# GpSimd's short operations between the two parts of a step's scalings, and a free-axis sum in place of an addition

## The chip, the cores and the metric

The kernel runs on one core of a Trainium2 chip. The time is what the device needs for one execution, in microseconds (us). The kernel before was timed in three executions: 1083.58, 1084.55 and 1084.83 us, median 1084.55 us. One more execution was profiled; it took 1084.76 us, and the span of its own instructions is 1083.0 us. The granted TensorE clock was 0.999 in it.

## The reference

Eight batches of eight heads of causal attention with a decay, and then a feed-forward layer with a gate on the 4608 tokens that result:

```python
def _attn_ref(q, k, v, f):              # 8 x 8 x 576 x 64
    scores = scale * np.matmul(q, k.transpose(0, 1, 3, 2))
    cum = np.cumsum(np.log(np.clip(f, 0.0001, 1.0)), axis=-1)
    decay = cum[:, :, :, None] - cum[:, :, None, :]
    scores = np.where(causal, -1000000000.0, scores + decay)
    scores = scores - np.max(scores, axis=-1, keepdims=True)
    attn = np.exp(scores)
    attn = attn / (np.sum(attn, axis=-1, keepdims=True) + 1e-09)
    return np.matmul(attn, v)

def _moe_ref(x, w_in, w_out):           # 4608 x 512, 512 x 2048, 2048 x 512
    h = x @ w_in
    sp = np.maximum(h, 0.0) + np.log1p(np.exp(-np.abs(h)))
    return (h * erf(sp)) @ w_out
```

The attention's output, heads side by side, is the x of the layer.

## The kernel before

The first part of the program, about 340 us, is the attention; the rest is the layer, in 48 units that the change doesn't touch. The order of the instructions on every engine is the order in which the code names them.

**Steps.** The heads are taken in 32 pairs, each pair in two steps, so t runs from 0 to 63, with two more in which the pipeline empties. A head's 576 rows of scores are cut into five blocks of rows; an even step has blocks 4 and 1 (576 and 192 columns), an odd step blocks 3, 2 and 0 (448, 320 and 64 columns), each for both heads j of the pair. A tile of step t goes through five stages, one step apart:

- step t: `scores(t)` puts the products on TensorE (PE) into PSUM; a matrix on `upper` adds the causal mask to the rows' ends. `reduce(t, j)` (L559, VectorE, DVE) adds the decay `c`, writes `pr` and keeps each row's smallest value in `st[:, 0]`. The next step's `scores` needs the PSUM that `reduce` reads, of both heads.
- step t+1: `exps` (L571, ScalarE, ACT) writes the exponentials over `pr` and their sums into `st[:, 1]`.
- step t+2: `normalize` adds 1e-9 to the sums (L576, DVE), takes the reciprocal (L578, DVE), and GpSimd (POOL) scales each block by it (L582), large blocks first.
- step t+3: `transposes` (PE) turns `pr` in groups of up to four squares into one of three PSUM buffers `t`, and `evacuate` copies them to `pt` (ACT, and DVE for one group of an odd tile). For an odd tile the group with block 0 is turned first.
- step t+4: `values` (PE) multiplies with v into `o`, of which there is one buffer; one step later `store` (L630 and L633, DVE) copies it to `xo`, and a DMA writes it to `xt_d`. PE's `values` of a step waits for the `store` of the step's own round, which DVE does ahead of its `reduce`.

So PE's order in a step is s (scores of t), t (transposes of t-3), o (values of t-4), and DVE's is sums and reciprocal of t-2, store of t-5, reduce of t, and then the conversions.

**GpSimd's other work.** `mask(p, i)` (L546) writes a large negative value into a piece of the decay `c`. The one of block 4, for the next pair, stands in odd steps. The one of block 3, in even steps, overwrites columns that `reduce` of the same step has still to read, so it waits for DVE.

**Conversions.** Beside the attention the weights of the first units, and from step 23 on the first x, are cut into high and low parts. A list `work` with due times by step sets the pace, and `moe.later` that of x. Each entry, called by `convert` at the end of a step, has instructions on several engines: `words` and `joined` on DVE (L377 to L395, on 512 columns each), `out_high`, `in_high` and `high` on ACT (L401, L418, L138), and on GpSimd subtractions and additions of 256, 384 or 512 columns: `out_low` (L406), `combine` (L414), `in_low` (L424), `sub` (L132) and `low` (L143). These last are the short operations. `columns` counts GpSimd's columns of an entry. DMAs of the finished parts are issued on SyncE's queue (SP) ahead of the next entry.

Of the kernel before, what the change touches and what calls it, by code (L numbers as in the profile page):

```python
# [22 lines left out]
P = 128  # L23
# [38 lines left out]
X0 = 23  # L62
X1 = 60
BY_X0 = 17
NU1 = 4
# [5 lines left out]
EDGE = 24  # L71
# [243 lines left out]
def attention_moe(ctx, tc, q2, k2, vp, f, w_in, w_out, out):  # L315
# [19 lines left out]
    tiny = edge.tile([P, EDGE], F32, name="edge")  # L335
    nc.vector.memset(tiny, 1e-9)
# [124 lines left out]
    with ExitStack() as ph:  # L461
# [57 lines left out]
        def scores(t):  # L519
# [20 lines left out]
            line = wk.tile([P, 32], F32, name=f"st{t}", tag=f"st{half}")  # L540
            stats[t] = line[:, :6 * n].rearrange("p (a j m) -> p a j m", a=3, j=2)
# [32 lines left out]
        def normalize(t):  # L574
            st, n = stats.pop(t), len(BLOCKS[t % 2])
            nc.vector.tensor_tensor(out=st[:, 1], in0=st[:, 1], in1=tiny[:, :2 * n].rearrange("p (j m) -> p j m", j=2),  # L576
                                    op=ALU.add)
            nc.vector.reciprocal(out=st[:, 2], in_=st[:, 1])  # L578
            for m, i in enumerate(BLOCKS[t % 2]):
                for j in range(2):  # L580
                    seg = row(t, i, j)
                    nc.gpsimd.tensor_scalar(out=seg, in0=seg, scalar1=st[:, 2, j, m:m + 1], scalar2=1.0,  # L582
                                            op0=ALU.mult, op1=ALU.mult)

# [95 lines left out]
        for t in range(NH + 2):  # L680
# [13 lines left out]
            if there[2]:  # L694
                normalize(t - 2)
# [31 lines left out]
            if there[0] and not half:  # L727
                mask(p, 3)
            if t < 4:
                due = t + 1  # L730
            elif t <= X0:
                due = 4 + ((BY_X0 - 4) * (t - 3) + (X0 - 3) // 2) // (X0 - 3)
            else:
                due = BY_X0 + ((total - BY_X0) * (t - X0) + (X1 - X0) // 2) // (X1 - X0)
            while work and total - len(work) < due:
                done += columns(work[0])
                convert(work.pop(0))
            if t == X0:
                begun = done
            for _ in range(2 if t > X0 else 0):  # L740
                if moe.later and done < begun + (every - begun) * (t - X0) // (X1 - X0):
                    done += columns(moe.later[:1])
                    convert(moe.later[:1])
                    del moe.later[:1]
            if t > NH and there[4]:
                store(t - 4)
# [81 lines left out]
```

## Time and profile before

| | before |
|---|---|
| median of three executions | 1084.55 us |
| profiled execution, its own time | 1084.76 us |
| span of its instructions | 1083.0 us |
| PE busy in the span | 1071.5 us (99%) |
| DVE busy | 834.7 us (77%) |
| ACT busy | 745.7 us (69%) |
| GpSimd busy | 732.0 us (68%) |

Times in the rows are us from the start of the span, durations are us too, and nanoseconds where the view says so. A row of the timeline gives the start, the duration, the engine, the line, the operation, what it writes and reads, and how many instructions were merged into it; in square brackets stands how long the engine had been idle before it, and what ended that. PE's matmuls are pipelined and their ends are modelled, so PE's busy share hides its waits: an s row that waits in its midst is shown as a longer row.

### The profile page before, as it was taken

Reading aid. Unit: us, or ns where it says so; the run is one execution under the profiler, and the core shown is the slowest. Engines: PE = TensorE matmul, PEld = TensorE weight load, DVE = VectorE, ACT = ScalarE, POOL = GpSimd, SP = SyncE. Lnnn points to the kernel's source line nnn. Section 1 sums busy time; section 2 is a strip of 40 time slices with the busy share of each in tenths; the row PEclk is TensorE's granted clock in tenths of the full one; section 3 lists DMA queues with packets and bytes.
Section 4 is the critical chain, followed back from the end, with each engine's and each line's share of the span. In section 5 each row is a group of like instructions: output and inputs, shape, how many; then the busy total and the mean of one; then the engine's idle time right before and its main releaser. Section 6 shows DMA issues by size and latency. Waiting matters only on the chain.

```text
span 1083.0 us, 21938 instructions
## 1 busy us (share of the span) xinstructions
PE 1071.5 (99%) x7480; PEld 945.5 (87%) x7480; DVE 834.7 (77%) x1875; ACT 745.7 (69%) x1624; POOL 732.0 (68%) x887
## 2 busy tenths in 40 slices
PE   8999999999999999999999999999999999999998
PEld 6888887888889988998899888989998999899987
DVE  6898898888765997888887986685776768676665
ACT  5899888988987666657666666566476656656563
POOL 3777888988864969798787879636454555536322
PEclk9999999999999999999999999999999999999999
DMA  8799987899766597877969777785867768584742
GB/s 285 247 304 311 343 305 251 279 351 350 254 215 226 190 349 280 303 299 287 357 221 364 273 270 271 277 295 204 311 230 264 289 221 323 213 319 182 246 188 97
DMA packets 86191, 293.69 MB, mean 271 GB/s; under 512 B 8896, under 2 KB 25280, under 8 KB 73792
## 3 DMA queue, kind: packets, MB, share of 16 engines
q1 hardware_dynamic: 85936, 292.00, 75.9%
q8 instruction: 60, 0.98, 0.3%
q14 instruction: 51, 0.42, 0.1%
q10 hardware_dynamic: 144, 0.29, 0.1%
HBM read 240.73 MB, written 51.53 MB: 270 GB/s over the span
## 4 chain that ended last, share of the span: by engine, by line
PE 87%; DVE 4%; ACT 3%; DMA 3%; issue 1%; POOL 1%; SPq 0%; DVEq 0%; POOLq 0%; ACTq 0%
PE y L236 34%; PE pha L178 9%; PE phx L178 9%; PE phy L178 9%; PE s L528 7%; PE o L621 7%; PE t L594 5%; PE phb L178 4%; DMA xt_d<-xo 2%; ACT pr L571 1%; PE s L535 1%; POOL pr L582 1%; DVE pr L559 1%; DMA v<-in_vp_dram 1%; ACT pt L603 1%
## 5 line engine op out<-in xcount | busy, mean ns | idle before, releaser
L225 POOL TENSOR_TENSOR gl<-e,gh 128x384 fp32r<-128x384 f32 x192 | 218.2, 1168 | 262.7 <-PE y L236 162.4
L236 PE MATMUL y<-wo,gh 128*128 128x512 f32 x1152 | 356.5, 391 | 0.4 <-DVE ys L257 0.3
L236 PEld LDWEIGHTS y<-wo,gh 128*128 128x128 f32 x1152 | 215.0, 188 | 45.4 <-DVE ys L257 1.7
L236 PE MATMUL y<-wo,gl 128*128 128x512 f32 x576 | 225.1, 391 | 0.0
L257 DVE TENSOR_TENSOR ys<-y,ys 128x512 f32<-128x512 f32 x252 | 172.1, 687 | 55.2 <-PE y L236 53.6
L582 POOL TENSOR_SCALAR pr<-pr,st 128x576 f32<-128x576 f32 (+4 forms) x320 | 167.6, 544 | 49.2 <-ACT pt L603 11.9
L571 ACT ACTIVATE pr<-pr,st 128x576 f32<-128x576 f32 (+3 forms) x320 | 177.1, 560 | 2.2 <-DVE st L559 2.2
L559 DVE CUSTOM_DVE_ANT_0 pr<-s,c 128x576 f32<-128x576 f32 (+3 forms) x320 | 136.6, 487 | 40.9 <-PE s L535 18.4
L224 ACT CAST gh<-e 128x384 fp32r<-128x384 f32 x192 | 94.1, 513 | 67.3 <-DVE e L217 64.9
L207 ACT ACTIVATE e<-u 128x384 f32<-128x384 f32 x144 | 75.0, 523 | 78.2 <-DVE u L184 74.9
L236 PEld LDWEIGHTS y<-wo,gl 128*128 128x128 f32 x576 | 108.1, 188 | 22.8
L178 PE MATMUL pha<-xs,wi 128*128 128x384 f32 x576 | 117.0, 337 | 0.1
L178 PE MATMUL phx<-xs,wi 128*128 128x384 f32 x576 | 115.4, 334 | 0.0
L178 PE MATMUL phy<-xs,wi 128*128 128x384 f32 x576 | 115.3, 334 | 0.0
L528 PE MATMUL s<-k,q 64*128 64x320 f32 (+4 forms) x768 | 113.8, 407 | 1.5 <-DVE st L559 1.1
L603 ACT COPY pt<-t 128x512 f32<-128x512 f32 x158 | 88.6, 582 | 33.5 <-PE t L594 33.4
L207 ACT ACTIVATE e<-pha 128x384 f32<-128x384 f32 x48 | 23.6, 492 | 125.7 <-PE pha L178 125.7
L621 PEld LDWEIGHTS o<-pt,v 128*64 128x64 f32 x1920 | 93.7, 137 | 14.2 <-DVE st L559 6.9
L178 PEld LDWEIGHTS pha<-xs,wi 128*128 128x128 f32 x576 | 102.3, 188 | 4.2 <-DVE u L188 0.4
L621 PE MATMUL o<-pt,v 128*64 128x128 f32 (+1 forms) x1920 | 102.5, 259 | 3.1 <-DVE xo L630 2.9
L528 PEld LDWEIGHTS s<-k,q 64*128 64x128 f32 x768 | 75.0, 186 | 31.3 <-issue 16.0
L594 PE MATMUL t<-ident,pr 128*128 128x128 f32 x800 | 100.9, 275 | 1.3 <-ACT pt L599 0.9
(75 smaller groups left out, 1780.5 us busy)
## 6 DMA issues: line engine op xcount, KB each, us to landing
wi<-wi_d SPq DMA_DIRECT2D x48, 1792.0 KB, 7.5
wo<-wo_d SPq DMA_DIRECT2D x48, 1024.0 KB, 5.6
v<-in_vp_dram SPq DMA_DIRECT2D x32, 576.0 KB, 5.2
r<-xt_d SPq DMA_DIRECT2D x48, 384.0 KB, 8.9
c<-cum_d SPq DMA_DIRECT2D x62, 288.0 KB, 6.9
q<-in_q_dram SPq DMA_DIRECT2D x32, 320.0 KB, 5.7
k<-in_k_dram SPq DMA_DIRECT2D x32, 288.0 KB, 6.0
part_d<-ys SPq DMA_DIRECT2D x36, 256.0 KB, 6.0
```

Source lines behind the costliest of these rows:

```text
L178: nc.tensor.matmul(out=ps, lhsT=wi[:, w, n, kd], rhs=xs[:, x, kd], start=not part and kd == 0 and i == 0, stop=kd == 1 and i == 2, skip_gr ...
L207: nc.scalar.activation(out=e_, in_=h[c], func=AF.Softplus)
L225: nc.gpsimd.tensor_tensor(out=gl, in0=e_, in1=gh.bitcast(F32), op=ALU.subtract)
L236: nc.tensor.matmul(out=y, lhsT=x[:, cs], rhs=wo[:, i, w], start=i == 0 and n == 0, stop=i == 1 and n == 2)
L257: nc.vector.tensor_tensor(out=ys, in0=y, in1=ys, op=ALU.add)
L528: nc.tensor.matmul(out=s[j][:, at:at + k1 - k0], lhsT=q[h, PAD + START[i]:PAD + END[i]], rhs=k[h, k0:k1], start=i > 0, stop=k1 < END[i] or ...
L559: nc.vector.tensor_tensor_reduce(out=to[:, ::-1] if j else to, in0=score, in1=decay_, scale=-0.125, scalar=BIG, op0=ALU.add, op1=ALU.min, ...
L571: nc.scalar.activation(out=seg, in_=seg, func=AF.Exp, bias=st[:, 0, j, m:m + 1], scale=-1.0, accum_out=st[:, 1, j, m:m + 1])
L582: nc.gpsimd.tensor_scalar(out=seg, in0=seg, scalar1=st[:, 2, j, m:m + 1], scalar2=1.0, op0=ALU.mult, op1=ALU.mult)
L594: nc.tensor.transpose(out=b[:, n * P:(n + 1) * P], in_=probs[t][:, at:at + P], identity=ident)
L603: nc.scalar.copy(out=pt[:, 512 * a:512 * a + 512], in_=b)
L621: nc.tensor.matmul(out=o[h, to:to + width], lhsT=v[:, ch, h], rhs=pt[:, at[j]:at[j] + width], start=n == 0, stop=n == len(parts) - 1, skip ...
```

## The change

Two things are changed. The constant 1e-9 now stands beside the sums in the same tile `line`, and one instruction that sums over two neighbouring places (a tensor reduce along the free axis, on sums and constant) takes the place of the addition of two tiles. Four fixed tiles are used in turn, where a pool gave four before. And `normalize` is cut in two: the sums, the reciprocal and the large block (576 or 448 columns, both heads) stay at the start of a step; the smaller blocks come at its end. Where a step's entries have at most 640 columns (`SHORT`) for GpSimd, they are called ahead of block 3's mask and of the smaller blocks; otherwise behind them. Entries of x are no longer taken in the step in which their high part is made.

```diff
-    tiny = edge.tile([P, EDGE], F32, name="edge")
-    nc.vector.memset(tiny, 1e-9)
+    lines = [edge.tile([P, 2, 6 * len(BLOCKS[n % 2])], F32, name=f"line{n}") for n in range(4)]
+    for line in lines:
+        nc.vector.memset(line[:, 1], 1e-9)
...
-            line = wk.tile([P, 32], F32, name=f"st{t}", tag=f"st{half}")
-            stats[t] = line[:, :6 * n].rearrange("p (a j m) -> p a j m", a=3, j=2)
+            stats[t] = lines[t % 4][:, 0, :6 * n].rearrange("p (a j m) -> p a j m", a=3, j=2)
...
-        def normalize(t):
-            st, n = stats.pop(t), len(BLOCKS[t % 2])
-            nc.vector.tensor_tensor(out=st[:, 1], in0=st[:, 1], in1=tiny[:, :2 * n].rearrange("p (j m) -> p j m", j=2),
-                                    op=ALU.add)
-            nc.vector.reciprocal(out=st[:, 2], in_=st[:, 1])
-            for m, i in enumerate(BLOCKS[t % 2]):
+        def normalize(t, rest):
+            half = t % 2
+            st, n = stats[t], len(BLOCKS[half])
+            total = st[:, 2].rearrange("p j m -> p (j m)")
+            if not rest:
+                nc.vector.tensor_reduce(out=total, in_=lines[t % 4][:, :, 2 * n:4 * n].rearrange("p w c -> p c w"),
+                                        axis=mybir.AxisListType.X, op=ALU.add)
+                nc.vector.reciprocal(out=total, in_=total)
+            for m in range(n - 1, 0, -1) if rest else range(1):
                 for j in range(2):
-                    seg = row(t, i, j)
+                    seg = row(t, BLOCKS[half][m], j)
                     nc.gpsimd.tensor_scalar(out=seg, in0=seg, scalar1=st[:, 2, j, m:m + 1], scalar2=1.0,
                                             op0=ALU.mult, op1=ALU.mult)
+            if rest:
+                del stats[t]
...
-                normalize(t - 2)
+                normalize(t - 2, False)
...
-            if there[0] and not half:
-                mask(p, 3)
...
+            todo = []
             while work and total - len(work) < due:
-                done += columns(work[0])
-                convert(work.pop(0))
+                todo.append(work.pop(0))
...
             for _ in range(2 if t > X0 else 0):
-                if moe.later and done < begun + (every - begun) * (t - X0) // (X1 - X0):
-                    done += columns(moe.later[:1])
-                    convert(moe.later[:1])
+                last = todo[-1][0][0] if todo and todo[-1] else None
+                if last != moe.high and moe.later and (
+                        done + sum(map(columns, todo)) < begun + (every - begun) * (t - X0) // (X1 - X0)):
+                    todo.append(moe.later[:1])
                     del moe.later[:1]
+            now = sum(map(columns, todo))
+            done += now
+            for late in (False, True):
+                if late == (now > SHORT):
+                    for steps in todo:
+                        convert(steps)
+                if not late and there[0] and not half:
+                    mask(p, 3)
+                if not late and there[2]:
+                    normalize(t - 2, True)
```

Lines of the changed kernel are a few higher than those of before (L585 is L582 of before, L579 stands for L576, L581 for L578, L407 for L406, and so on). The order of the instructions of PE, ACT and SyncE stays as it was; on DVE one instruction for one is replaced, and three small fills are added at the start.

GpSimd in steps 20 and 21, before: pr18 and pr19 are the tiles that are scaled there, c10 and c11 the decays that are masked, and the rows with wtop5 and wa1 are the short operations of the two steps.

```order
L582 TENSOR_SCALAR pr18_1562<-pr18_1562,st18_1563 128x576 x2
L582 TENSOR_SCALAR pr18_1562<-pr18_1562,st18_1563 128x192 x2
L546 AFFINE_SELECT c10_1375<-c10_1375 128x2x128
L406 TENSOR_TENSOR wtop5_1201<-wtop5_1201,wohi1_1_1614 128x512
L582 TENSOR_SCALAR pr19_1642<-pr19_1642,st19_1643 128x448 x2
L582 TENSOR_SCALAR pr19_1642<-pr19_1642,st19_1643 128x320 x2
L582 TENSOR_SCALAR pr19_1642<-pr19_1642,st19_1643 128x64 x2
L546 AFFINE_SELECT c11_1538<-c11_1538 128x2x128
L414 TENSOR_TENSOR wa1_1772<-wa1_1772 128x256
```

The same two steps on GpSimd in the changed kernel:

```order
L585 TENSOR_SCALAR pr18_1548<-pr18_1548,line2_82 128x576 x2
L407 TENSOR_TENSOR wtop5_1193<-wtop5_1193,wohi1_1_1596 128x512
L546 AFFINE_SELECT c10_1365<-c10_1365 128x2x128
L585 TENSOR_SCALAR pr18_1548<-pr18_1548,line2_82 128x192 x2
L585 TENSOR_SCALAR pr19_1625<-pr19_1625,line3_83 128x448 x2
L546 AFFINE_SELECT c11_1526<-c11_1526 128x2x128
L415 TENSOR_TENSOR wa1_1752<-wa1_1752 128x256
L585 TENSOR_SCALAR pr19_1625<-pr19_1625,line3_83 128x64 x2
L585 TENSOR_SCALAR pr19_1625<-pr19_1625,line3_83 128x320 x2
```

In the even step the short operation moved up ahead of the mask, and the two scalings of 192 columns moved behind both. In the odd step mask and short operation moved ahead of the four smaller scalings, and block 0 (64 columns) now comes ahead of block 2 (320). Of the steps with short operations, 29 are made so (15 even, 14 odd).

GpSimd in steps 26 and 27, before; the two subtractions of 512 columns are together over 640 columns:

```order
L582 TENSOR_SCALAR pr24_2057<-pr24_2057,st24_2058 128x576 x2
L582 TENSOR_SCALAR pr24_2057<-pr24_2057,st24_2058 128x192 x2
L546 AFFINE_SELECT c13_1865<-c13_1865 128x2x128
L424 TENSOR_TENSOR wa1_1772<-wa1_1772,whi1_0_2109 128x512 x2
L582 TENSOR_SCALAR pr25_2144<-pr25_2144,st25_2145 128x448 x2
```

The same place in the changed kernel:

```order
L585 TENSOR_SCALAR pr24_2037<-pr24_2037,line0_80 128x576 x2
L546 AFFINE_SELECT c13_1849<-c13_1849 128x2x128
L585 TENSOR_SCALAR pr24_2037<-pr24_2037,line0_80 128x192 x2
L425 TENSOR_TENSOR wa1_1752<-wa1_1752,whi1_0_2085 128x512 x2
L585 TENSOR_SCALAR pr25_2121<-pr25_2121,line1_81 128x448 x2
```

Here the short operations stay at the end of the step; only the mask and the 192-column scalings changed places. There are 13 such steps.

DVE at the end of step 30 and the start of step 31, before; pr31 is the tile that `reduce` makes there, o26 the one that `store` copies:

```order
L377 TENSOR_SCALAR wtop10_2605<-wraw10_2114 128x512
L378 TENSOR_SCALAR wtop10_2605<-wtop10_2605 128x512
L379 TENSOR_SCALAR wtop10_2605<-wtop10_2605 128x512
L576 TENSOR_TENSOR st29_2473<-st29_2473,edge_80 128x6
L578 RECIPROCAL st29_2473<-st29_2473 128x6
L630 COPY xo13_2621<-o26_2578 128x2x128
L559 ISA pr31_2635,st31_2636<-s31_0_2623,c15_2199 128x448
```

The same place on DVE in the changed kernel:

```order
L378 TENSOR_SCALAR wtop10_2580<-wraw10_2090 128x512
L379 TENSOR_SCALAR wtop10_2580<-wtop10_2580 128x512
L380 TENSOR_SCALAR wtop10_2580<-wtop10_2580 128x512
L579 TENSOR_REDUCE line1_81<-line1_81 128x6
L581 RECIPROCAL line1_81<-line1_81 128x6
L635 COPY xo13_2592<-o26_2551 128x2x128
L559 ISA pr31_2606,line3_83<-s31_0_2594,c15_2179 128x448
```

Only the addition became a reduction, at the same place, behind the conversions of its step and ahead of the store and the reduce of the next.

More of the change, by code (lines that the diff above doesn't have):

```diff
@@ L64 @@
 BY_X0 = 17
+SHORT = 640
 NU1 = 4
@@ L69 @@
 MASK = -2.0 ** 33
-EDGE = 24
 BIG = 3.0e38
@@ L734, in attention_moe @@
                 due = BY_X0 + ((total - BY_X0) * (t - X0) + (X1 - X0) // 2) // (X1 - X0)
+            todo = []
             while work and total - len(work) < due:
-                done += columns(work[0])
-                convert(work.pop(0))
+                todo.append(work.pop(0))
             if t == X0:
-                begun = done
+                begun = done + sum(map(columns, todo))
             for _ in range(2 if t > X0 else 0):
-                if moe.later and done < begun + (every - begun) * (t - X0) // (X1 - X0):
-                    done += columns(moe.later[:1])
-                    convert(moe.later[:1])
+                last = todo[-1][0][0] if todo and todo[-1] else None
+                if last != moe.high and moe.later and (
+                        done + sum(map(columns, todo)) < begun + (every - begun) * (t - X0) // (X1 - X0)):
+                    todo.append(moe.later[:1])
                     del moe.later[:1]
+            now = sum(map(columns, todo))
[8 more added lines that the diff above has]
+                    normalize(t - 2, True)
             if t > NH and there[4]:
```

## The prediction

> **What bounds the kernel now.** I read the page first, then a table of busy time by stretches, then PE's timeline for the steps of the attention, and then, at each step that is longer than a clean one, DVE's and GpSimd's.
>
> ```profile
> PE 87%; DVE 4%; ACT 3%; DMA 3%; issue 1%; POOL 1%; SPq 0%; DVEq 0%; POOLq 0%; ACTq 0%
> 29.60:320.60 291.00, 286.92 (x3399) 240.41 (x3395) 244.75 (x899) 257.59 (x788) 238.69 (x418) 1.00 0.87 292
> 301.69 1.56 PE L528 MATMUL s<-k,q 64*128 64x320 f32 x12
> 306.30 1.73 PE L528 MATMUL s<-k,q 64*128 64x448 f32 x12
> 311.17 1.56 PE L528 MATMUL s<-k,q 64*128 64x320 f32 x12
> ```
>
> PE bounds the kernel: 87% of the chain that ended last is its own work. GpSimd has 1% of that chain, so less work on GpSimd is worth nothing by itself; the change can only shorten waits of PE. The third row is the stretch from step 5 to step 63, the one that the change touches: 291.0 us. The three s rows are a clean pair of steps: 4.61 us for the even one, 4.87 for the odd, 9.48 together. The stretch holds 29 pairs and an odd step, 29 x 9.48 + 4.87 = 279.8 us. **So PE waits 11.2 us in it in all, and no gain can be larger.** Where these waits lie:
>
> ```profile
> 47.40 1.54 PE L621 MATMUL o<-pt,v 128*64 128x128 f32 x28 [0.20 <-DVE xo L634]
> 48.87 2.15 PE L528 MATMUL s<-k,q 64*128 64x448 f32 x12
> 63.65 1.78 PE L528 MATMUL s<-k,q 64*128 64x320 f32 x12
> 110.74 1.66 PE L621 MATMUL o<-pt,v 128*64 128x128 f32 x32 [0.58 <-DVE xo L630]
> 112.33 2.23 PE L528 MATMUL s<-k,q 64*128 64x320 f32 x12
> 131.99 2.10 PE L528 MATMUL s<-k,q 64*128 64x320 f32 x12
> 141.23 1.66 PE L621 MATMUL o<-pt,v 128*64 128x128 f32 x32 [0.74 <-DVE xo L630]
> 142.82 2.23 PE L528 MATMUL s<-k,q 64*128 64x320 f32 x12
> 162.50 2.02 PE L528 MATMUL s<-k,q 64*128 64x320 f32 x12
> 183.22 2.23 PE L528 MATMUL s<-k,q 64*128 64x320 f32 x12
> 222.84 2.23 PE L528 MATMUL s<-k,q 64*128 64x320 f32 x12
> 253.17 2.06 PE L528 MATMUL s<-k,q 64*128 64x320 f32 x12
> PE o L621 <- DVE xo L630: 2.6, 4, 0.9
> DVE xo L630 <- DMA xt_d<-xo: 2.7, 1, 2.7
> 246.24 0.66 PE L594 MATMUL t<-ident,pr 128*128 128x128 f32 x4 [0.61 <-ACT pt L599]
> ```
>
> An s row above 1.56 (even) or 1.73 (odd) waited for DVE's reduce of the step before: 0.42, 0.22, 0.67, 0.54, 0.67, 0.46, 0.67, 0.67 and 0.50, together 4.8 us. The o rows waited for DVE's store: 0.20, and 2.6 in four other steps. That is 7.6 us in which **DVE was late**. Most of the other 3.6 us are waits for ACT's copies, of which the last row is the longest: ACT's order isn't changed, so I leave them. At step 44 a store waited for a DMA (2.7 us), which the change doesn't touch: 0.67 and a share of the 2.6 stay.
>
> **The addition becomes a reduction.**
>
> ```profile
> L576 DVE TENSOR_TENSOR st<-st,edge x64: 149/165/1390, 17.8 to 327.8; 128x4 f32<-128x4 f32 x32, 128x6 f32<-128x6 f32 x32
> L578 DVE RECIPROCAL st<-st x64: 178/186/193, 18.0 to 328.0; 128x4 f32<-128x4 f32 x32, 128x6 f32<-128x6 f32 x32
> 158.86 1.23 DVE L576 TENSOR_TENSOR st<-st,edge 128x6 f32<-128x6 f32 x1
> ```
>
> The first two rows give the shortest, median and longest time in ns. The addition of four or six columns takes 149 ns, but up to 1390; the reciprocal, with one input of the same size, never leaves 178 to 193. At 158.86 the addition ended only when a short operation of GpSimd did. So an instruction with one input doesn't meet GpSimd here, and one with two does. The reduction has one input. Its own length isn't in the trace: I take 0.18 us, the reciprocal's; between 0.15 (the addition unhindered) and 1.39 (held as long as the addition at worst, which is the second rival). The 0.02 us that it is longer than the median addition are hidden in the idle time of DVE, busy for 244.75 of the 291.0 us. On the path this is worth one place: the 1.23 at 158.86 falls by 1.05 us, which is more than the 0.46 that PE waits at 162.50. **Gain 0.46.** Elsewhere the held additions fall in steps in which PE doesn't wait for DVE.
>
> The Trainium skill, "SBUF — State Buffer", section "Who interferes with whom", says that a DVE instruction with two SBUF inputs contends with a GpSimd instruction that reads SBUF, and that a tensor reduce on this chip never contends. The two L576 and L578 rows agree for the first half; no run here shows a reduction yet. If the second half failed, the gain just named would be 0.
>
> **The short operations move ahead of the smaller scalings.** DVE's conversions stand at the end of a step, and GpSimd's short operations stood there too:
>
> ```profile
> 43.40 1.23 DVE L386 SCALAR_TENSOR_TENSOR wtop<-wraw,wtop 128x512 int32<-128x512 int32 x1
> 58.68 0.94 DVE L377 TENSOR_SCALAR wtop<-wraw 128x512 int32<-128x512 int32 x1
> 106.58 1.48 DVE L386 SCALAR_TENSOR_TENSOR wtop<-wraw,wtop 128x512 int32<-128x512 int32 x1
> 105.86 0.41 POOL L546 TENSOR_SCALAR_AFFINE_SELECT c<-c 128x256 f32<-128x256 f32 x1 [1.30 <-DVE st L559]
> 106.23 1.28 POOL L406 TENSOR_TENSOR wtop<-wtop,wohi 128x512 f32<-128x512 f32 x1
> 108.70 0.42 DVE L377 TENSOR_SCALAR wtop<-wraw 128x512 int32<-128x512 int32 x1
> 126.96 1.20 DVE L386 SCALAR_TENSOR_TENSOR wtop<-wraw,wtop 128x512 int32<-128x512 int32 x1
> 136.90 2.71 DVE L377 TENSOR_SCALAR wtop<-wraw 128x512 int32<-128x512 int32 x1
> 176.82 1.48 DVE L386 SCALAR_TENSOR_TENSOR wtop<-wraw,wtop 128x512 int32<-128x512 int32 x1
> 247.54 1.17 DVE L386 SCALAR_TENSOR_TENSOR wtop<-wraw,wtop 128x512 int32<-128x512 int32 x1
> 202.24 0.69 DVE L386 SCALAR_TENSOR_TENSOR wtop<-wraw,wtop 128x512 int32<-128x512 int32 x1
> 202.36 1.48 POOL L582 TENSOR_SCALAR pr<-pr,st 128x64 f32<-128x64 f32 x2
> 41.87 0.60 POOL L582 TENSOR_SCALAR pr<-pr,st 128x64 f32<-128x64 f32 x2
> ```
>
> At 106.58 L386 began 0.35 us after GpSimd's L406 and took 1.48 instead of the 0.69 of 202.24. From there DVE ran without a gap into the store that PE awaited at 110.74. In an even step the short operation will start behind the 576-column scalings, in the 1.30 us in which GpSimd now idles until DVE lets the mask go (the bracket at 105.86), and run beside DVE's reduce. What DVE's conversion meets instead is a scaling. The last three rows show such a meeting: L386 keeps 0.69, and GpSimd's two scalings of 64 columns take 1.48 instead of the 0.60 at 41.87. Step by step, with what DVE lost to GpSimd, what PE lost, and what I take:
>
> - step 7: DVE 1.23 - 0.69 = 0.54, PE 0.62; a 320-column scaling may hold L386 instead: 0.3.
> - step 10: DVE 0.94 - 0.42 = 0.52, PE 0.22: 0.22.
> - step 20: DVE 0.79, PE 1.25; the two 192-column scalings may hold it up to 0.4: 0.55.
> - step 24 (640 columns, two short operations): DVE 0.51 in the row shown, PE 0.54; part of the second operation still meets it: 0.35.
> - step 26 (1024 columns, so still late): DVE 2.71 - 0.42 = 2.29, PE 1.41. The mask now waits for DVE and the 192-column scalings come behind it, so the two operations start about 0.5 us later, and the row's L377 gets through ahead of them; what follows it may not: 0.8.
> - step 48: DVE 0.48, PE 0.50: 0.4.
> - step 34 (896 columns, late): DVE 0.79 at 176.82, PE 0.67 and a share of the 2.6: 0.
>
> Together 2.62; with nothing but the upper ends, the smaller of DVE's and PE's loss each, 0.54 + 0.22 + 0.79 + 0.51 + 1.41 + 0.48 = 3.95; the lower end is 0, if scalings hold DVE as long as short operations do.
>
> A second rule of that section, that whoever starts first holds the shared port for its whole instruction and the other blocks fully, speaks against the change: a conversion that comes second would wait for each scaling. By it each of the five gains at steps 7 to 48 could lose the length of one scaling. The row at 136.90 agrees with the blocking, the row at 202.24 shows the other order.
>
> **What the change adds.** The smaller scalings come later, and PE's transposes of the next step wait for them.
>
> ```profile
> 108.65 1.51 PE L594 MATMUL t<-ident,pr 128*128 128x128 f32 x12
> 190.73 3.29 POOL L582 TENSOR_SCALAR pr<-pr,st 128x448 f32<-128x448 f32 x6 [1.80 <-DVE st L578]
> 194.54 1.54 POOL L414 TENSOR_TENSOR wa<-wa 128x256 f32<-128x256 f32 x2
> 194.98 1.59 PE L594 MATMUL t<-ident,pr 128*128 128x128 f32 x13
> ```
>
> Even steps, by step 20: the mask goes at 105.86 at the earliest, ends at 106.27, and two scalings of some 0.42 end at 107.1. PE needs block 1 in the last four of the twelve transposes from 108.65, at 109.6. The margin is 2.5 us. Odd steps, at the tightest place I found: the six scalings from 190.73, the mask's 0.41 and two operations of 1.54 end at 190.73 + 3.29 + 0.41 + 1.54 = 195.97; block 2 is needed seven transposes after 194.98, at 195.84. That would cost 0.1. Block 0 is ready earlier than that, since it comes first. A short operation that now comes early could wait for its source: ACT's high parts are made a step earlier, and x entries are held back behind them, so I cost it at nothing; if it did wait, the scalings behind it use up those margins first. On SP nothing moves, and the DMAs of finished parts can only be ready earlier. I take 0.3 for all of this, between 0 and 1.0.
>
> **Sum.** 0.46 + 2.62 - 0.3 = 2.8 us. The profiled execution goes from a span of 1083.0 to 1080.2, from its own 1084.76 to 1082.0; the median, 0.21 lower, from 1084.55 to 1081.8 us. What a measurement of this kernel can tell from no change is about 0.2%, 2.2 us, so the line is at 1082.4.
>
> **Rivals.**
> - *Scalings hold DVE as long as the short operations did.* For it: 136.90, where a conversion waited through two operations in a row; against it: 202.24. Only the addition's 0.46 stays: 1084.1 us.
> - *The reduction meets GpSimd as the addition did*, so that half of the change doesn't do what it says: 1084.55 - 2.62 + 0.3 = 1082.2 us. Against it stands the reciprocal's row.
> - *DVE is freed wholly.* All DVE stalls but those of step 44 (about 1.1) go: 1084.55 - 6.5 = 1078.0 us. Against it: 13 steps keep the late order.
> - *Slower: PE waits for the smaller scalings of odd steps.* DVE's conversions hold them: the two at 202.36 took (1.48 - 0.60) / 2 = 0.44 us more each than the two at 41.87. Four scalings so held are 1.8 late. If the margins of the 14 odd steps with early operations are spread evenly between 0 (step 37) and the 2.5 of step 20, the 1.8 reach 10 of them and cost each 0.9 in the mean, 9 us at worst; if half of the four are held, 0.9 late, 5 steps of 0.45, 2 us. I take the middle, 5.5 us: 1084.55 - 2.8 + 5.5 = 1087.2 us. It decides from the point at which block 2 ends over 0.85 us (seven transposes) after the transposes begin.
>
> **Chances.** The forecast 0.57, with a range of its own from 1079.9 (the upper ends of the list) to 1083.3 (half of what I take); of that, 0.48 lies below 1082.4. The first rival 0.27, the second 0.03, the third 0.05, the slower one 0.08. Faster: 0.48 + 0.03 + 0.05 = 0.56; within 0.2%: 0.09 + 0.27 = 0.36; slower 0.08. The range that should hold the time 8 times in 10 takes in the forecast's and the first rival's time with the measurement's spread, and leaves out the third and the slower one: 1079.3 to 1084.9.
>
> **What would show it.** L579's longest time is near its shortest; DVE's L387 and L378 in steps 7, 10, 20 and 48 are near 0.69 and 0.42; the s rows of steps 12, 22, 26, 32 and 50 come near 1.56; POOL's scalings become longer, not DVE's conversions; the wait of PE's transposes for GpSimd stays near nothing; steps 36 and 44 keep their stalls. I am wrong if DVE's conversions keep their stretched rows, if PE's t rows gain idle time before them that GpSimd ended, or if freed DVE time only moves PE's wait to ACT's copies.

## The result and the profile after

The changed kernel takes 1092.01 us (median of four executions, 1091.38 to 1093.01), the kernel before 1084.07 us in the same measurement. The ratio is 1.0074, with a 95% interval of 1.0056 to 1.0091: slower by 8 us. The profiled execution took 1093.01 us, its span is 1091.2 us.

The attention first. These are the rows of PE's timeline after the change in which an s group (clean: 1.56 or 1.73 us) waited for `reduce`:

```profile
49.21 2.12 PE L529 MATMUL s<-k,q 64*128 64x448 f32 x12
111.75 2.19 PE L529 MATMUL s<-k,q 64*128 64x320 f32 x12
141.05 1.81 PE L529 MATMUL s<-k,q 64*128 64x320 f32 x12
160.26 1.90 PE L529 MATMUL s<-k,q 64*128 64x320 f32 x12
181.24 2.23 PE L529 MATMUL s<-k,q 64*128 64x320 f32 x12
206.00 2.00 PE L529 MATMUL s<-k,q 64*128 64x448 f32 x12
216.48 2.15 PE L529 MATMUL s<-k,q 64*128 64x448 f32 x12
222.87 2.23 PE L529 MATMUL s<-k,q 64*128 64x320 f32 x12
237.62 1.96 PE L529 MATMUL s<-k,q 64*128 64x448 f32 x12
```

and these are the rows of its view of waits for the o groups (us in all, times, longest):

```profile
PE o L626 <- DVE xo L635: 2.3, 2, 1.3
PE o L626 <- DVE xo L639: 0.6, 1, 0.6
```

The waits of steps 12, 26 and 50 are gone, step 28's (141.05) fell from 0.67 to 0.25. What remains at 49.21 (step 9), 111.75 (22), 181.24 (36) and 222.87 (44) is nearly as before; 206.00 and 216.48 (41 and 43) are new, and the o groups wait 2.9 us where they waited 2.8. So the attention gained and gave a part back. Its length from step 5's first matmul to the layer's first y is read from these rows of PE's timeline, of before:

```profile
29.64 1.73 PE L528 MATMUL s<-k,q 64*128 64x448 f32 x12
346.67 0.63 PE L236 MATMUL y<-wo,gh 128*128 128x512 f32 x2
```

and of the changed kernel:

```profile
30.25 1.73 PE L529 MATMUL s<-k,q 64*128 64x448 f32 x12
346.12 0.62 PE L236 MATMUL y<-wo,gh 128*128 128x512 f32 x2
```

317.03 us became 315.87: 1.2 faster. But from the first y to the end of the span there are 1083.0 - 346.67 = 736.3 us before and 1091.15 - 346.12 = 745.0 us now (the page rounds that span to 1091.2). **The loss is 8.7 us in the layer, in which no instruction was changed.** One of its units in PE's timeline, before:

```profile
760.62 1.23 PE L178 MATMUL pha<-xs,wi 128*128 128x384 f32 x6
...
767.93 0.63 PE L236 MATMUL y<-wo,gh 128*128 128x512 f32 x2
...
776.13 1.23 PE L178 MATMUL pha<-xs,wi 128*128 128x384 f32 x6
```

and after:

```profile
763.91 1.23 PE L178 MATMUL pha<-xs,wi 128*128 128x384 f32 x6
...
771.22 0.62 PE L236 MATMUL y<-wo,gh 128*128 128x512 f32 x2
...
779.65 1.23 PE L178 MATMUL pha<-xs,wi 128*128 128x384 f32 x6
```

The 42 matmuls of the first product take 7.31 us in both. The 36 matmuls that write y take 8.20 us before and 8.43 now: 228 and 234 ns from the start of one to the start of the next, without a gap. The groups of the page say the same of all 1728, before:

```profile
L236 PE MATMUL y<-wo,gh 128*128 128x512 f32 x1152 | 356.5, 391 | 0.4 <-DVE ys L257 0.3
L236 PE MATMUL y<-wo,gl 128*128 128x512 f32 x576 | 225.1, 391 | 0.0
```

and after:

```profile
L236 PE MATMUL y<-wo,gh 128*128 128x512 f32 x1152 | 363.3, 396 | 0.0
L236 PE MATMUL y<-wo,gl 128*128 128x512 f32 x576 | 228.2, 396 | 0.0
```

Each is 5 ns longer in the mean. These durations overlap, so the time is lost in the distance from one start to the next: over all y matmuls that follow one another within 0.4 us, its mean went from 228.6 to 234.3 ns. That is 9.8 us for 1728 of them; the rest of the layer became 1.1 us shorter. PE's busy share is 99% in both pages and the granted clock 1.00, so nothing that looks like a wait gives it away. In the y matmuls gh and gl are the weights, and wo is the operand that streams.

What the change did do to the layer is to move its tiles. The four fixed tiles take 512 bytes of each partition where the constant took 96, and the pools of the right side are laid out below them: q, k and c, and later u, e, gh and gl. All of these start 416 bytes lower. In the built programs gh and gl start at a multiple of 128 bytes before, and 96 bytes beside one after. wo lies on the other side and didn't move.

### The profile page after: what moved, and what is told of

Same layout as the page of the kernel before. It is cut to its first block, busy times and chain, and to the rows that moved or that the text cites. A ratio compares the mean times of both kernels' runs of the same rounds, so it can differ in the third digit from the quotient of the medians.

```text
span 1091.2 us, 21938 instructions
## 1 busy us (share of the span) xinstructions
PE 1080.0 (99%) x7480; PEld 947.3 (87%) x7480; DVE 839.5 (77%) x1878; ACT 745.8 (68%) x1624; POOL 737.7 (68%) x887
## 4 chain that ended last, share of the span: by engine, by line
PE 93%; ACT 2%; DVE 2%; DMA 1%; POOL 1%; issue 0%; SPq 0%; POOLq 0%; ACTq 0%; DVEq 0%
PE y L236 37%; PE pha L178 9%; PE phy L178 9%; PE phx L178 9%; PE s L529 8%; PE o L626 8%; PE t L599 6%; PE phb L178 5%; ACT pr L571 1%; DMA xt_d<-xo 1%; PE s L536 1%; DVE pr L559 1%; ACT pt L608 1%; PE lead L502 1%; POOL pr L585 0%
## 5 line engine op out<-in xcount | busy, mean ns | idle before, releaser
L236 PE MATMUL y<-wo,gh 128*128 128x512 f32 x1152 | 363.3, 396 | 0.0
L236 PEld LDWEIGHTS y<-wo,gh 128*128 128x128 f32 x1152 | 216.0, 188 | 48.9 <-DVE ys L257 0.4
L236 PE MATMUL y<-wo,gl 128*128 128x512 f32 x576 | 228.2, 396 | 0.0
L585 POOL TENSOR_SCALAR pr<-pr,line 128x576 f32<-128x576 f32 (+4 forms) x320 | 174.4, 567 | 38.9 <-DVE line L581 15.0
L571 ACT ACTIVATE pr<-pr,line 128x576 f32<-128x576 f32 (+3 forms) x320 | 177.1, 561 | 2.3 <-DVE line L559 2.3
L236 PEld LDWEIGHTS y<-wo,gl 128*128 128x128 f32 x576 | 108.5, 188 | 26.6
L217 DVE TENSOR_TENSOR e<-e,u 128x384 f32<-128x384 f32 x144 | 117.1, 814 | 0.0
L178 PEld LDWEIGHTS phx<-xs,wi 128*128 128x128 f32 x576 | 101.2, 188 | 0.0
```

The costliest lines, as they stand in the source:

```text
L178: nc.tensor.matmul(out=ps, lhsT=wi[:, w, n, kd], rhs=xs[:, x, kd], start=not part and kd == 0 and i == 0, stop=kd == 1 and i == 2, skip_gr ...
L217: nc.vector.tensor_mul(e_, e_, h_)
L236: nc.tensor.matmul(out=y, lhsT=x[:, cs], rhs=wo[:, i, w], start=i == 0 and n == 0, stop=i == 1 and n == 2)
L571: nc.scalar.activation(out=seg, in_=seg, func=AF.Exp, bias=st[:, 0, j, m:m + 1], scale=-1.0, accum_out=st[:, 1, j, m:m + 1])
```

## The experiments

Two theories. A, placement: gh and gl lie badly, so each y matmul takes longer. B, order: the layer starts in another phase between DVE and GpSimd. For B speaks that DVE's L217 (e times u) takes 820 ns in the mean instead of 686. Its rows in the stretch from 340 us on, before and after:

```profile
L217 DVE TENSOR_TENSOR e<-e,u 128x384 f32<-128x384 f32 x142 | 97.4, 686 | 0.0
L217 DVE TENSOR_TENSOR e<-e,u 128x384 f32<-128x384 f32 x141 | 115.6, 820 | 0.0
```

Four sets of kernels, in the order in which they ran. "layer" is the time from the first y to the end of the span in each kernel's profile, "y" is the mean duration of the y matmuls with gh and with gl as weights, from the rows of L236 in each kernel's profile (L239 in the one with gl alone moved), "place" where the tiles start modulo 128 bytes in the built program, and the ratio is against the kernel before on the same chip, with its 95% interval. Each set ran on another chip, on which the kernel before took 1084.27, 1085.09, 1084.48 and 1084.33 us; so sets are compared by the ratio and by the layer, not by the time.

| run | code | place of gh, gl | us | ratio | layer, us | y, ns |
|---|---|---|---|---|---|---|
| before | before | 0 | 1084.07 | | 736.3 | 391, 391 |
| changed | changed | 96 | 1092.01 | 1.0074 (1.0056 to 1.0091) | 745.0 | 396, 396 |
| e1 | changed | 64 | 1089.87 | 1.0052 (1.0040 to 1.0065) | 743.5 | 394, 394 |
| e2 | before | 96 | 1093.03 | 1.0081 (1.0068 to 1.0095) | 743.5 | 395, 395 |
| e3 | order alone | 64 | 1092.36 | 1.0074 (1.0062 to 1.0087) | 743.4 | 394, 394 |
| e4 | reduction alone | 64 | 1091.47 | 1.0068 (1.0055 to 1.0080) | 743.4 | 394, 394 |
| e5 | changed | 0 | 1081.86 | 0.9970 (0.9958 to 0.9982) | 735.9 | 390, 391 |
| e6 | changed, packed | 0 | 1082.48 | 0.9971 (0.9959 to 0.9982) | 736.1 | 390, 391 |
| e7 | order alone | 0 | 1085.34 | 1.0001 (0.9992 to 1.0009) | 736.0 | 390, 391 |
| e8 | reduction alone | 0 | 1084.45 | 0.9995 (0.9987 to 1.0004) | 736.3 | 390, 391 |
| e9 | packed | 0; u, e at 96 | 1082.17 | 0.9979 (0.9970 to 0.9988) | 735.9 | 390, 391 |
| e10 | packed | 32; u, e at 0 | 1090.44 | 1.0053 (1.0039 to 1.0067) | 743.5 | 396, 396 |
| e11 | packed | gh 0, gl 32 | 1089.84 | 1.0044 (1.0031 to 1.0057) | 742.1 | 397, 390 |
| e12 | packed, all early | 0 | 1081.26 | 0.9971 (0.9959 to 0.9982) | 735.3 | 390, 391 |
| e13 | packed | 0; wo, ys at 64 | 1083.73 | 0.9993 (0.9985 to 1.0002) | 737.2 | 393, 389 |
| e14 | packed | 64; wo, ys at 64 | 1087.10 | 1.0025 (1.0016 to 1.0034) | 740.9 | 395, 394 |
| e15 | packed | 0; q, k, c moved | 1081.84 | 0.9976 (0.9966 to 0.9986) | 735.7 | 390, 391 |

### First set: the tiles back to 64 bytes, and the kernel before moved away

e1 is the changed kernel with one unused tile:

```diff
+    edge.tile([P, 8], F32, name="pad")
```

> The changed kernel with 32 unused bytes more in the pool of the four fixed tiles, so that the layer's u, e, gh and gl (and the attention's q, k, c) start again at multiples of 64 bytes in a partition, as before the change; instructions and their order are the changed kernel's. Theory A (placement: the 1728 y matmuls of the layer take 234.4 ns from start to start instead of 229.0 because gh and gl start 32 bytes beside a multiple of 64): y back at 227 to 231 ns, time 1083.5 us (1082.5 to 1084.2), what the attention alone gained in the one profile being 0.5 us. Theory B (the changed order of the attention leaves the layer in another phase between VectorE and GpSimd, seen in L217's mean of 820 ns instead of 686, and this costs the 8 us): 1092 us as the changed kernel, y still at 234 ns.

e2 is the kernel before with its tiles moved as the change moved them:

```diff
-EDGE = 24
+EDGE = 32
-            line = wk.tile([P, 32], F32, name=f"st{t}", tag=f"st{half}")
+            line = wk.tile([P, 24], F32, name=f"st{t}", tag=f"st{half}")
```

> The kernel before, with the tile of the constant 128 bytes instead of 96 (and the st tiles 96 instead of 128 for room), so that u, e, gh, gl, q, k and c start 32 bytes beside a multiple of 64; instructions and order are those of before. Theory A: y matmuls at 234 ns from start to start, 1084.1 + 8.7 = 1092.8 us (1091 to 1094). Theory B: 1084 us, y at 229 ns.

e3 is e1 with the addition in place of the reduction, e4 the kernel before with lines and reduction of the changed kernel and the unused tile of e1:

```diff
-                nc.vector.tensor_reduce(out=total, in_=lines[t % 4][:, :, 2 * n:4 * n].rearrange("p w c -> p c w"),
-                                        axis=mybir.AxisListType.X, op=ALU.add)
+                w = lines[t % 4][:, :, 2 * n:4 * n]
+                nc.vector.tensor_tensor(out=total, in0=w[:, 0], in1=w[:, 1], op=ALU.add)
```

> The first kernel of this set with the reduction taken back to an addition of two inputs (sums and constant of the same tile): the new order of GpSimd alone, on 64-byte places. Prediction's own steps (2.62 for the order less 0.3, 0.46 for the reduction): 1084.1 - 2.3 = 1081.8 us, 0.5 slower than with the reduction; if the one profile of the changed kernel is typical (its attention ends 0.5 us earlier, gains of 2 us until step 41 are lost again at steps 42 and 43): 1083.6 to 1084.5 us; additions of L576's kind up to 1.4 us long again.

> The kernel before with the reduction in place of the addition, on 64-byte places, GpSimd's order as before. The prediction's step: the reduction never longer than 0.25 us, and 0.46 us gained at step 32: 1083.6 us (1083.2 to 1084.1). If a reduction contends like the addition: 1084.1 us with single reductions over 1 us.

e2 settles A against B: the kernel before, with no instruction replaced or reordered (one fill at the start has 32 columns instead of 24), takes 1093.03 us as soon as its tiles are moved. Its layer is 743.5 us long, which is 7.2 of the changed kernel's 8.7 us; gh and gl lie 96 bytes beside a multiple of 128 in both, and where the other 1.5 us come from stays open. e1 didn't come out as expected: I had taken 64 bytes for the unit, and its y matmuls stayed at 394 ns. e3 and e4, whose expectations rested on the same unit, came out at least 7 us above them. e4 has GpSimd's old order and is slow too, so the order isn't needed for the loss.

### Second set: the same place as before

e5, e7 and e8 are e1, e3 and e4 with a larger unused tile, which puts gh and gl 512 bytes below their old place, at the same place modulo 512:

```diff
-    edge.tile([P, 8], F32, name="pad")
+    edge.tile([P, 24], F32, name="pad")
```

> The changed kernel with 96 unused bytes more beside the four fixed tiles, so that gh, gl, u and e start 512 bytes lower than before the change, at the same place modulo 512 (384). Placement theory, in its second form (64 bytes aren't enough: 32, 64 and 96 modulo 128 are all slow, 0 is fast): y matmuls back at 229 ns from start to start with 227 for most of a unit, L217's mean back at 690 ns, time 1082.5 us (1081.5 to 1083.7: the time before less the 0.6 to 2.4 us by which the layer's first y begins earlier in the profiles of the changed kernel and of the aligned one). Rival (only the absolute address of before is fast, or the speed isn't bound to the address): 1090 to 1092 us, y at 233 or 234.

e6 packs the four tiles, and so reaches another multiple of 128; the packed lines are the base of all later kernels:

```diff
-    lines = [edge.tile([P, 2, 6 * len(BLOCKS[n % 2])], F32, name=f"line{n}") for n in range(4)]
+    lines = [edge.tile([P, 4, 2 * len(BLOCKS[n % 2])], F32, name=f"line{n}") for n in range(4)]
```

> The changed kernel with the four fixed tiles packed (min, sum, constant, reciprocal one behind the other, 320 bytes in all) and 32 unused bytes, so that gh, gl, u and e start at 128 modulo 512. If a multiple of 128 is what counts: as the kernel at 384 modulo 512, y at 229 ns or less, 1082.5 us. If the place against the other operand wo (at 128 modulo 512) counts: y at 233 ns or another number, 1087 to 1092 us.

> GpSimd's new order with the addition of two inputs, gh and gl at 384 modulo 512. By the prediction's terms 1084.1 - 2.62 + 0.3 = 1081.8 us; from the set before (order alone 2.5 us slower than order and reduction): 1085 us (1084 to 1086) beside the 1082.5 of order and reduction at this place. If placement isn't the cause of the 8 us: 1092 us.

> The reduction alone, GpSimd's order as before, gh and gl at 384 modulo 512. By the prediction's term 1083.6 us; from the set before (reduction alone 1.6 us slower than order and reduction): 1084.1 us (1083.3 to 1085). If placement isn't the cause of the 8 us: 1091.5 us.

With the tiles at a multiple of 128 the same instructions are **faster** than before: 0.9970. The layer of e5 begins with this row of its timeline

```profile
343.56 0.63 PE L236 MATMUL y<-wo,gh 128*128 128x512 f32 x2
```

and lasts 1079.5 - 343.56 = 735.9 us, as before the change. Its L217 is back at 687 ns, so DVE's longer rows go with the place of the tiles and not with the order. The two parts alone bring nothing that the time shows (e7, e8), both together 0.3%. For e8 that is no surprise, since 0.46 us was expected of it. For e7 2.3 us was; why they are missing shows in its timelines of GpSimd and DVE at step 26, one of the steps in which the short operations stay late:

```profile
137.43 2.85 POOL L426 TENSOR_TENSOR wa<-wa,whi 128x512 f32<-128x512 f32 x2
```

```profile
137.78 1.38 DVE L381 TENSOR_SCALAR wtop<-wtop 128x512 int32<-128x512 int32 x1
139.08 1.23 DVE L581 TENSOR_TENSOR line<-line 128x6 f32<-128x6 f32 x1
140.46 0.42 DVE L636 COPY xo<-o 128x256 f32<-128x256 f32 x1
```

The first short operation holds a conversion (1.38 instead of 0.43), the second the addition (1.23), and the store that PE awaits comes behind both. Before, L377 had waited through both (2.71). With the new order and the reduction, only the first of the two waits is left:

```profile
135.95 0.42 DVE L378 TENSOR_SCALAR wtop<-wraw 128x512 int32<-128x512 int32 x1
136.41 0.54 DVE L379 TENSOR_SCALAR wtop<-wtop 128x512 f32<-128x512 f32 x1
136.98 1.38 DVE L380 TENSOR_SCALAR wtop<-wtop 128x512 int32<-128x512 int32 x1
```

(the changed kernel's DVE at the same step). In e8 L379, the same conversion as L377 of before, takes 2.71 us there, as before.

### Third set: which tiles, and all steps early

One unused tile inside the layer's pool moves u and e against gh and gl, or gl against gh; in e10 and e11 the pad of the edge pool is left out. The line of e9 and e10:

```diff
         moe.activate(0)
+        moe.ep.tile([P, 8], F32, name="gap", bufs=1)
```

> The changed kernel with gh and gl (what the y matmuls load as weights) at a multiple of 128 bytes, and u and e (what VectorE's L217 and ScalarE read and write) 32 bytes beside one. Theory W (y is slow because of where its own weights lie): y at 229 ns from start to start, 1082.5 us (1081.5 to 1083.5). Rival V (the operands of VectorE or ScalarE lie badly, and their traffic slows PE's reading): y at 233 to 235 ns, 1091 us.

> The reverse: u and e at a multiple of 128 bytes, gh and gl 32 bytes beside one (q, k and c too, as in the changed kernel). Theory W: y at 233 to 235 ns, 1082.5 + 8.7 = 1091 us (1090 to 1092.5). Rival V: 229 ns, 1082.5 us.

> Only gl beside a multiple of 128 (gl is the weight of every third y matmul, 576 of 1728). If each badly placed weight slows its own or its neighbour's matmul: one of three intervals is 15 or so ns longer or all three by 2, 1082.5 + 8.7/3 = 1085.4 us (1084 to 1087). If one badly placed weight in three already spoils the rhythm of all: 1090 us, as with all. If only gh matters: 1082.5 us.

With u and e beside a multiple of 128 nothing is lost (e9), with gh and gl beside one nearly all of it (e10). L217 goes along: 684 ns in e9, where its own tiles lie badly, and 807 in e10, where they lie well. The idle time before PE's y rows is 0.4 us in all in e9 and 0.1 in e10, so PE doesn't wait for it; why it becomes longer wasn't tried. e11 moves gl alone, and its rows are the most telling ones:

```profile
L239 PE MATMUL y<-wo,gh 128*128 128x512 f32 x1152 | 363.7, 397 | 0.1
L239 PE MATMUL y<-wo,gl 128*128 128x512 f32 x576 | 224.5, 390 | 0.0
```

The matmuls with gl, whose weights lie badly, are as short as ever; the ones with gh are longer. Each gl matmul stands behind two of gh, and its weights are loaded while the second of them runs. The mean times from start to start say where the loss is paid: from the second gh to gl 237.6 ns (228.2 in e5), from the first gh to the second 232.8 (227.9), and from gl to the next gh 228.9 (229.0). So the matmul that uses the badly placed weights pays nothing, and the one beside which they are loaded pays most. The 5 ns of the first gh, beside which well placed weights are loaded, this doesn't explain. Moving gl also moves what GpSimd writes, and no run separates that from PE's loads; but the loss falls on the neighbours of gl's loads, which speaks for the loads. I had expected a third of the loss or all of it; with a third of the weights moved it was nearly all (1089.84).

e12 calls the short operations early in all steps:

```diff
-SHORT = 640
+SHORT = 4096
```

> The changed kernel with tiles at multiples of 128 and SHORT at 4096, so that in the 13 steps with over 640 columns the short operations come ahead of the smaller scalings too. If VectorE's conversions that meet short operations at the end of those steps are what is left to gain (steps 34 to 36 wait 2.3 us in the kernel at the same place as before): 1080.5 us. If PE then waits for smaller scalings that come up to 2.5 us later (slack of 0.1 to 1.4 us in most odd steps with them early): 1084 us or more, with t rows that wait for POOL. I hold the second for likelier: 1084 (1081 to 1088).

1081.26 us, the lowest time of all, but its interval is that of e5 and e6: no difference can be told. The wait of PE for scalings that I held for likelier does appear, in step 14 of its timeline,

```profile
75.36 1.78 PE L600 MATMUL t<-ident,pr 128*128 128x128 f32 x13 [0.40 <-POOL pr L586]
```

but hardly elsewhere (its view of waits has 0.4 us of it in all, and 0.9 of PE's weight loads), and it is paid for by shorter waits for DVE (o for L636: 0.4 us in all, 1.3 in e5, most of it at step 35).

### Fourth set: the place, or the distance to wo; and q, k, c

e13 puts wo (and with it ys, which PE doesn't read) 64 bytes higher, e14 also moves gh and gl to 64 (the larger pad of e5); e15 moves only the attention's loads:

```diff
+    moe.wop.tile([P, 16], F32, name="gap", bufs=1)
     moe.load_wo(0)
```

```diff
             c = io.tile([P, 2, S], F32, name=f"c{p}", tag="c")
+            if not p:
+                io.tile([P, 8], F32, name="gap", bufs=1)
```

> The kernel with packed fixed tiles and gh, gl at a multiple of 128, with wo (and ys) 64 bytes higher, at 64 modulo 128. If the place of the weights itself counts: y at 229 ns from start to start, 1082.4 us (1081.4 to 1083.4). If the distance of the weights from wo counts, or if wo has to start at a multiple of 128 too: y at 233 ns or more, 1090 us.

> wo, gh and gl all 64 bytes beside a multiple of 128. If the place of the weights itself counts: y at 233 to 234 ns, 1090 us (1089 to 1091.5), as with gh and gl alone so placed. If the distance to wo counts: 229 ns, 1082.4 us.

> The kernel with packed fixed tiles, gh, gl, u, e at multiples of 128, and q, k, c of the attention 32 bytes beside a multiple of 64, as in the changed kernel. If their place costs the attention something: the first y of the layer at 345.5 to 346.1 us and 1083.5 to 1084.5 us. If not: the first y at 343.6 to 344.8 us and 1082.3 us (1081.3 to 1083.3). With a spread of about 1 us between runs the time alone may not tell; the span to the first y and the number of longer steps of PE should.

With wo and the weights shifted alike (e14) y stays slow, so the distance alone doesn't decide. But the place of the weights alone doesn't either: e14's layer is 740.9 us long, where it is 743.5 in e1 with the weights at the same 64 bytes and wo at 0, and its 1087.10 us lie between the two forecasts. With wo alone moved (e13) y is at 393 and 389 ns and the layer at 737.2; the time is 1.9 us above that of e15 on the same chip. So the streaming operand's place counts as well, but less, and the fastest of these placements has both at a multiple of 128. Neither expectation foresaw that. q, k and c cost nothing that shows in the time of e15. Its first y, at 345.29 us, lies between the two forecasts for it, so what their place does to the attention stays open.

## Why the prediction was wrong

- **What failed** is a step that the prediction never wrote down: it treats "the stretch from step 5 to step 63" as "the one that the change touches", and carries the layer's 736 us over unchanged into the sum ("from a span of 1083.0 to 1080.2"). The place of the tiles it put at nothing without a reason. The 416 bytes by which the four fixed tiles are larger than the constant moved every tile of the right side, and the y matmuls went from 228.6 to 234.3 ns from start to start: 8.7 us in the layer, a term that is absent from the sum, from the rivals and from the range. e2 shows 7.2 us of it without the rest of the change, e5 the rest of the change without it.
- **The sum for the attention** came out, in part by luck. Where the tiles lie as before (e5) the ratio is 0.9970, 3.2 us, where 2.8 us is 0.9974; that the time of 1081.86 us is nearly the 1081.8 of the forecast is chance, since the kernel before took 1085.09 on that chip. Step by step, from the start of one s group to the next, e5 against before, the waits caused at steps 7, 10, 20, 24, 26 and 48 fell by 0.33, 0.22, 0.50, 0.53, 1.23 and 0.46 us, where 0.3, 0.22, 0.55, 0.35, 0.8 and 0.4 was taken. The reduction brought 0.14 instead of 0.46, and step 35, taken as unchanged, became 0.38 longer; the surplus of step 26 makes up for that.
- **The reduction** behaves as forecast. The row of DVE in the changed kernel (shortest, median and longest, ns):

```profile
L579 DVE TENSOR_REDUCE line<-line x64: 145/156/168, 17.9 to 327.3; 128x4 f32<-128x8 f32 x32, 128x6 f32<-128x12 f32 x32
```

  It was never held, though 32 of the 64 lie wholly inside an instruction of GpSimd; the addition took up to 1390. That agrees with the half of the rule in the Trainium skill ("SBUF — State Buffer", section "Who interferes with whom") that no run had shown. The prediction's own reason, that an instruction with one input doesn't meet GpSimd here, is too wide: L377 at 136.90 has one input and took 2.71 instead of 0.42. Alone (e8) the reduction makes the s row of step 32 a clean one, so the whole 0.46 is there:

```profile
162.57 1.57 PE L530 MATMUL s<-k,q 64*128 64x320 f32 x12
```

  In the changed kernel it was 0.12 (the s row at 160.26 is still 0.34 above a clean one), since a late short operation now holds a conversion there.
- **The order** moved the meetings as forecast. DVE's conversions of steps 7, 10, 20, 24 and 48 in the changed kernel, and GpSimd's 192-column scalings of step 20:

```profile
44.01 0.72 DVE L387 SCALAR_TENSOR_TENSOR wtop<-wraw,wtop 128x512 int32<-128x512 int32 x1
58.85 0.42 DVE L378 TENSOR_SCALAR wtop<-wraw 128x512 int32<-128x512 int32 x1
106.66 0.68 DVE L387 SCALAR_TENSOR_TENSOR wtop<-wraw,wtop 128x512 int32<-128x512 int32 x1
126.47 0.92 DVE L387 SCALAR_TENSOR_TENSOR wtop<-wraw,wtop 128x512 int32<-128x512 int32 x1
247.40 0.73 DVE L387 SCALAR_TENSOR_TENSOR wtop<-wraw,wtop 128x512 int32<-128x512 int32 x1
```

```profile
106.32 1.31 POOL L585 TENSOR_SCALAR pr<-pr,line 128x192 f32<-128x192 f32 x2
106.72 0.91 POOL L585 TENSOR_SCALAR pr<-pr,line 128x192 f32<-128x192 f32 x1
```

  (the second row is the second scaling of the pair alone), and a pair of such scalings unhindered, in e7:

```profile
49.49 0.82 POOL L586 TENSOR_SCALAR pr<-pr,line 128x192 f32<-128x192 f32 x2
```

  The conversion began at 106.66, as the first scaling ended and 0.07 us ahead of the second. It kept its 0.68, and the second scaling became longer: 0.91 instead of about 0.42. So this agrees with the second rule of that section of the Trainium skill, that whoever comes first blocks the other for its whole instruction; the prediction feared it for the case in which the scaling comes first. Of the conversions shown, the one at 126.47 lost most, 0.23. Step 26 came out larger than taken: 1.41 us of waits fell to 0.25, where 0.8 was taken, and as written the first conversion gets through and a later one doesn't (1.38 at 136.98).
- **The two terms don't add.** 2.62 for the order and 0.46 for the reduction were summed as if each stood alone. Alone the order gives nothing (e7), because in late steps the addition takes the wait that the conversion was spared: held for 1.23 us at 75.11 and at 139.08, it makes steps 14, 15, 27 and 28 of e7 2.1 us longer than in e5.
- **The smaller scalings** cost little: the view of waits of the changed kernel has one of PE's weight loads waiting for them from 29.6 us on, and two at step 4, ahead of the stretch that the prediction looked at, where the step became 0.43 us longer (0.3 was taken for all of this).

```profile
PEld t L599 <- POOL pr L585: 0.2, 1, 0.2
PEld t L599 <- POOL pr L585: 0.4, 2, 0.3
```

  The slower rival, which had this mechanism and 1087.2 us, ended on the right side for a reason that wasn't so.
- **Steps 41 to 43** gave 2.0 us back in the changed kernel's profile, and the prediction has no cost for them. Both 41 and 43 are steps with late short operations, and the conversions of DVE there, unhindered before (0.69 at 202.24, and 0.45), waited through two short operations in a row:

```profile
200.26 2.61 DVE L387 SCALAR_TENSOR_TENSOR wtop<-wraw,wtop 128x512 int32<-128x512 int32 x1
200.37 1.96 POOL L143 TENSOR_TENSOR xs<-rT,xs 128x384 fp32r<-128x384 f32 x2
210.55 2.75 DVE L378 TENSOR_SCALAR wtop<-wraw 128x512 int32<-128x512 int32 x1
210.50 2.52 POOL L425 TENSOR_TENSOR wa<-wa,whi 128x512 f32<-128x512 f32 x2
```

  The new waits of PE at 206.00 and 216.48 and the o group's 0.6 for L639 follow from these two rows, together 1.3 us. In e5 the same two conversions got through sooner:

```profile
199.58 0.69 DVE L388 SCALAR_TENSOR_TENSOR wtop<-wraw,wtop 128x512 int32<-128x512 int32 x1
209.59 0.98 DVE L379 TENSOR_SCALAR wtop<-wraw 128x512 int32<-128x512 int32 x1
```

  The other 0.7 us were lost by the o group at 221.28, behind a store that waited 3.0 us for a DMA (2.7 before, none in e5; 3.0 in e12 too, where the o group lost 0.4). What decides whether the conversions get through wasn't tried. These 2.0 us are most of the difference between the 1.2 us that the attention gained in this profile and the 3.1 in e5's (29.61 to 343.56 is 313.95 us). This profile is also the slowest of the changed kernel's four executions, and e5's the fastest of its five.

```profile
DVE xo L635 <- DMA xt_d<-xo: 3.0, 1, 3.0
```

- **Smaller slips of the prediction.** Its list of s rows leaves out the one at 237.59, which waited 0.39. And the bounds of the forecast's own range don't come out of its terms: the upper ends, 3.95 and 0.46, give 1080.1 us and not 1079.9, half of 2.8 gives 1083.2 and not 1083.3. Nothing above hangs on these.

## What to carry to other kernels

A change in the size of one long-lived tile moves every tile that is laid out behind it: compare the start addresses of all tiles of before and after, modulo 128 bytes, as one compares the order of instructions. Where a matmul's weights come from such a tile, an unused tile that brings it back costs a line; here it turned a loss of 0.74% into a gain of 0.30%. And two remedies against one contention aren't added: what one of them frees, the next instruction in the queue can lose.

## What the hardware showed that I hadn't expected

- y matmuls (128x128 fp32r weights, 512 columns) follow each other in 228 ns with weights at a multiple of 128 bytes in the partition, and in 233 to 234 ns at 32, 64 or 96 beside one (e10, e1, the changed kernel). With the streaming operand at 64 as well it was 232.4 ns (e14). The matmul beside which badly placed weights are loaded pays more than the one that uses them (e11). Why it is 128 bytes, these runs don't show; no other shape of matmul was tried.
- Such a loss is no wait: the intervals are even, PE counts as busy, the clock is at 1.00. Only the mean of the same instruction against the other profile shows it.
- DVE's L217 went from 686 to between 800 and 820 ns in the mean wherever gh, gl or both lay beside a multiple of 128, and stayed below 690 wherever they didn't, with its own operands moved or not (e9: 684).
- A conversion of DVE that meets two short operations of GpSimd in a row can wait through both: 2.71 us before at step 26, 2.61 and 2.75 in the changed kernel, for 0.42 to 0.69 us of work. In e5 one of these slipped in between.
